# Engines of 708 operations from a table, and the low parts of two weight pieces on VectorE

## The chip, the cores and the metric

The kernel runs on one core of a Trainium2 chip. The metric is the device time of one execution in microseconds, lower is better.

## The reference

Three layers follow each other: attention with rotary positions (4 batches, 8 heads, 576 positions, 64 wide), a dense layer with a leaky ramp (2304 tokens, 512 to 2048 and back), and a soft mixture of 8 experts with 4 slots each. Cut to what is computed:

```python
q_rot, k_rot = rotate(q), rotate(k)
attn = softmax(scale * q_rot @ k_rot.T)
x = (attn @ v) as 2304 x 512
h = x @ w_in                                    # 512 -> 2048, weights given in 64 bits
x = (maximum(h, 0) + alpha * minimum(h, 0)) @ w_out
logits = x @ phi                                # 32 slots
d = softmax over tokens; slot_input = d.T @ x
slot_out[e] = maximum(slot_input[e] @ w1[e], 0) @ w2[e]
out = softmax over slots(logits) @ slot_out
```

## The kernel before

All work is cut into 2803 operations, each a few instructions on one engine, made by `plan.op(engine, cost, due, function, needed operations, buffers taken, buffers used)`. What fixes the order is not the due times but a table: `ORDER` is a packed list of all operations, which `Plan.order` unpacks and which is then issued from front to back. So the table sets what stands in each engine's own list; an engine works its list strictly in order and waits by semaphores for the others. DMA transfers are issued from SyncE's list in the same way.

**Attention.** For each batch `b` and pair of heads `p`, `prep_qk` loads q and k, multiplies by cos and sin (`mul`, L334) and adds (`add`, `whole`). In batch 0 scores are plain fp32 products (L434); from batch 1 on q and k are split into an fp32r part (`hi`, L350 and L352), its rest (`lo`, L357 and L359) and copies to the other partitions (`spread`, L362). `row_events` treats 128 rows at a time: scores on TensorE (L434, L443 to L447), the row maxima on VectorE (`top`, L452), the exponential with its sum on ScalarE (`expo`, L457), a guard of 1e-9 added to the sum (L473), the reciprocal (L474), and the product of the row with it, the norm (`norm`, L497 and L498). Batch 0 then turns blocks on TensorE (L521, L572) with evacuations (`turned`, L531; `turned_c`, L576); later batches turn 32x32 blocks on VectorE (L508, L542) and take a round trip through memory (tile `sc`). `pv_events` multiplies by v (L604) and evacuates a scaled fp16 part (`evac_hi`, L614) and its rest (`evac_lo`, L617).

**Weights.** `prep_w` loads a piece of `w_in` (8 pieces, `which` 0) or of `w_out` (8, `which` 1), converts it from 64 bits to fp32 by three VectorE operations (L673, L675, L677), and for `w_in` finds its bound (L685) and writes a scaled fp16 part (`hi`, L688). The low part comes from TensorE in two halves: `split` makes a diagonal of the scale (`diag`, L244), multiplies fp32 and subtracts the fp16 part in PSUM (L250, L251, tile `rest`), and evacuates (L256).

**The dense layer.** `chunk_events` runs `mm1` (L766, 12 fp16 matmuls of 128x256 for one of 16 chunks of one of 9 blocks of 256 tokens), the negative ramp `below` (L774) and the join `act` (L779). Its logits (L803), transposes of `g` (L795) and slot sums (L958) follow. The first `mm1` needs the attention of a quarter of batch 0; from there on chunks and score rows alternate on TensorE.

**Buffers.** There are two score banks (`st`) and three others (`pm`) in PSUM; a score bank is free after `expo`, the bank of a chunk after `act`. The weights of the experts (`late_w` and the loads behind it) need the attention's buffers, which are given back when its last operation, a `pv`, is done.

In the quoted functions engine and operation are fixed: the norm on `nc.gpsimd`, `below`, `evac_hi` and the guard on `nc.scalar`.

## Time and profile before

| | us |
|---|---|
| median of 3 runs (lowest, highest) | 570.95 (568.36, 573.3) |
| the profiled execution | 566.88 |
| its span | 565.1 |
| TensorE busy | 531.3 |
| VectorE busy | 449.7 |
| ScalarE busy | 348.8 |
| GpSimd busy | 321.9 |

Busy is the time in which at least one instruction of an engine runs; TensorE's are pipelined, and their ends are modelled. The trace has one line for each instruction with its start and duration. fp32 matmuls appear as two records. TensorE's clock was granted in full (0.996 on average). "Idle before" names what ended an engine's wait.

### The profile page before, as it was taken

What the parts mean: (1) busy time and instruction counts of PE and PEld (TensorE: products, weight loads), DVE (VectorE), ACT (ScalarE), POOL (GpSimd) and SP (SyncE); (2) the same over time, 40 slices, a digit from 0 to 9 for tenths busy, and PEclk for the clock granted to TensorE, in tenths of its full rate; (3) what the DMA queues carried; (4) which work ended last, traced back from release to release, by engine and by line L of the source; (5) the groups of instructions that cost most, each with busy time, mean ns of one, the idle gap of its engine ahead of it and who ended that gap; (6) DMA issues with size and microseconds to landing.
All of it is one profiled execution on the core that took longest, in us unless ns stands there. A gap on an engine that the chain in (4) does not pass through costs nothing.

```text
span 565.1 us, 14815 instructions
## 1 busy us (share of the span) xinstructions
PE 531.3 (94%) x5770; PEld 394.9 (70%) x5770; DVE 449.7 (80%) x985; ACT 348.8 (62%) x879; POOL 321.9 (57%) x299
## 2 busy tenths in 40 slices
PE   3789998999999999999999999999999999999994
PEld 1455555678888787788787788868778888864463
DVE  5699978878998878889889798888864799843551
ACT  2799977899868767787786787667432222430131
POOL 0989996988989876887886787844300000001000
PEclk9999999999999999999999999999999999999998
DMA  8893945435899988698989789889665999899997
GB/s 300 309 361 118 328 123 181 135 119 167 293 337 333 332 282 314 194 333 287 327 294 339 252 287 319 266 262 327 226 227 179 411 407 406 290 372 391 403 327 226
DMA packets 80806, 160.76 MB, mean 284 GB/s; under 512 B 5344, under 2 KB 44640, under 8 KB 80736
## 3 DMA queue, kind: packets, MB, share of 16 engines
q1 hardware_dynamic: 79408, 158.99, 80.6%
q8 instruction: 46, 0.75, 0.5%
q10 hardware_dynamic: 1328, 0.82, 0.5%
q14 instruction: 24, 0.20, 0.1%
HBM read 115.75 MB, written 36.96 MB: 270 GB/s over the span
## 4 chain that ended last, share of the span: by engine, by line
PE 75%; ACT 3%; DVE 2%; DMA 1%; issue 1%; DVEq 0%; ACTq 0%
PE ph L766 33%; PE pv L604 11%; PE st L447 9%; PE pu L958 4%; PE lg L803 3%; PE ph L1289 2%; PE po L1348 2%; DMA ett<-sc 1%; PE st L443 1%; PE pf L1473 1%; PE st L445 1%; PE pt L521 1%; PE lgt L863 1%; ACT ks L362 1%; ACT e L457 1%
## 5 line engine op out<-in xcount | busy, mean ns | idle before, releaser
L766 PE MATMUL ph<-xt,w 128*128 128x256 f16 x1536 | 184.2, 273 | 0.5 <-DVE xt L617 0.5
L766 PEld LDWEIGHTS <-w 128*128 128x128 f16 x1728 | 161.9, 98 | 30.2 <-issue 7.4
L498 POOL TENSOR_SCALAR e<-e,mm 128x576 f32<-128x576 f32 x144 | 125.5, 881 | 70.3 <-DVE mm L474 66.7
L457 ACT ACTIVATE e<-st,mm 128x576 f32<-128x576 f32 x144 | 106.3, 739 | 37.1 <-DVE mm L452 31.3
L452 DVE TENSOR_REDUCE mm<-st 128x1 f32<-128x576 f32 x144 | 106.2, 742 | 20.1 <-PE st L447 11.7
L774 ACT ACTIVATE rl<-ph 128x256 f32<-128x256 f32 x144 | 53.5, 380 | 69.7 <-PE ph L766 63.9
L334 POOL TENSOR_TENSOR xn<-xn,tabs 128x576 f32<-128x576 f32 x60 | 89.4, 1502 | 6.9 <-DMA xn<-in_k_dram 3.0
L779 DVE SCALAR_TENSOR_TENSOR g<-rl,oma,ph 128x256 f32<-128x256 f32 x144 | 65.7, 465 | 21.3 <-ACT rl L774 20.6
L604 PE MATMUL pv<-ET,vt 128*64 128x256 f32 (+1 forms) x640 | 76.5, 384 | 0.1
L508 DVE STREAM_TRANSPOSE tb<-e 128x512 f32<-128x512 f32 (+1 forms) x108 | 74.8, 704 | 1.7 <-DMA sc<-tb 0.8
L447 PE MATMUL st<-ks,qs 128*128 128x288 f32 x384 | 74.6, 317 | 1.1 <-ACT ks L362 0.9
L604 PEld LDWEIGHTS pv<-ET,vt 128*64 128x64 f32 (+1 forms) x640 | 43.1, 136 | 25.8 <-issue 5.8
L447 PEld LDWEIGHTS st<-ks,qs 128*128 128x128 f32 x384 | 54.5, 189 | 4.6 <-issue 1.6
L795 DVE STREAM_TRANSPOSE gb<-g 128x512 f32<-128x512 f32 x64 | 43.9, 693 | 0.2
L434 PE MATMUL st<-ks 64*128 64x288 f32 (+1 forms) x168 | 30.2, 455 | 11.0 <-DVE ks L307 7.6
L978 POOL MEMSET edt<- 128x256 f32 x1 | 0.3, 313 | 68.4 <-DVE lp L947 68.4
L359 POOL TENSOR_TENSOR qs<-xn,qs 64x576 fp32r<-64x576 f32 x24 | 33.9, 1413 | 7.7 <-ACT qs L352 3.1
L337 POOL TENSOR_TENSOR xn<-xn 128x576 f32<-128x576 f32 x24 | 36.9, 1537 | 0.9
L362 ACT ACTIVATE ks<-xn 64x576 fp32r<-64x576 f32 x48 | 32.6, 680 | 0.7
L434 PEld LDWEIGHTS st<-ks 64*128 64x128 f32 (+1 forms) x168 | 17.2, 191 | 20.8 <-DVE ks L307 8.4
L614 ACT ACTIVATE xt<-pv,vb 128x256 f16<-128x256 f32 x32 | 15.1, 472 | 22.3 <-PE pv L604 21.5
L457 ACT ACTIVATION_READ_ACCUMULATOR e<-st,mm 128x1 f32 x144 | 28.5, 198 | 0.0
(171 smaller groups left out, 782.1 us busy)
## 6 DMA issues: line engine op xcount, KB each, us to landing
sc<-tb SPq DMA_DIRECT2D x48, 576.0 KB, 4.6
ET<-sc SPq DMA_DIRECT2D x24, 1152.0 KB, 7.3
xw<-in_moe_w_dram SPq DMA_DIRECT2D x42, 512.0 KB, 8.4
xn<-in_k_dram SPq DMA_DIRECT2D x15, 576.0 KB, 6.5
xn<-in_q_dram SPq DMA_DIRECT2D x15, 576.0 KB, 4.5
wraw<-in_moe_w_in_dram SPq DMA_DIRECT2D x8, 1024.0 KB, 8.4
wraw<-in_w_out_t_dram SPq DMA_DIRECT2D x8, 1024.0 KB, 6.0
wor<-in_moe_w_out_dram SPq DMA_DIRECT2D x16, 512.0 KB, 10.0
```

The lines of the kernel that those rows point to most:

```text
L334: eng.tensor_tensor(e["x"][:, w], e["x"][:, w], tabs[:, w], ALU.mult)
L434: nc.tensor.matmul(st[to, j, at:at + w], x, k[rows, z:z + w], start=True, stop=True)
L447: nc.tensor.matmul(st[:, j, 0:288], r["q"][:, 768 * h + 128 * s:768 * h + 128 * s + 128].bitcast(F32R), r["k"][:, a, h, ks].bitcast(F32R), ...
L452: nc.vector.tensor_reduce(c["mm"][:, h:h + 1], c["st", h][:, :, 0:288], axis=AX.XY, op=ALU.max, negate=True)
L457: nc.scalar.activation(c["e"][:, h].rearrange("p (a n) -> p a n", a=2), c["st", h][:, :, 0:288], AF.Exp, bias=c["mm"][:, h:h + 1], accum_o ...
L498: nc.gpsimd.tensor_scalar(c["e"][:, h], c["e"][:, h], c["mm"][:, 6 + h:7 + h], 1.0, ALU.mult, ALU.mult)
L508: nc.vector.transpose(out=to if tail else to[:, :, 0:8].rearrange("p q (m h) j -> p q m h j", h=2)[:, :, :, h], in_=e.rearrange("p (m q j) ...
L604: nc.tensor.matmul(pv[r], v[k, 4 * h + i if i < 4 else 8 + (h if b else 0)], x, start=(i == 0), stop=(i == 4))
L766: nc.tensor.matmul(ph, wi[j][:, wp, kc, 128 * fo:128 * fo + 128], xt[:, xp, kc, :], start=(n == 0), stop=(n == 3 * KC - 1),)
L774: nc.scalar.activation(c["r"], c["ph"], AF.Relu, scale=-1.0)
L779: nc.vector.scalar_tensor_tensor(blk["g", j][:, fo, :], c["r"], oma[:, f:f + 1], c["ph"], ALU.mult, ALU.add)
L795: nc.vector.transpose(out=blk["gt", j // 2][:, f % 8 - 1:f % 8 + 1, :].rearrange("p c n -> p (c n)"), in_=blk["g", j][:, fo - 1:fo + 1, :] ...
```

## The change

A second table, `ENGINES`, holds one digit for each of 708 operations. `Plan.choose` takes the next digit and returns one of the engines that the call offers; `copied` and `times` write a copy or a product for whichever engine it is. So the following operations, which had one engine each, get the table's: diagonals and results of the splits, rotation products and sums, `hi`, `lo` and `spread` of q and k, guards, norms, the evacuations of the turned blocks, `evac_hi`, the scaled part of a `w_in` piece, and `below`. `ORDER` is a new list for the operations as they now are. Of the pieces of `w_in`, the last two (`j >= 6`) have no `split`: one VectorE operation (`lo` in `prep_w`, L747) multiplies the whole piece by its scale and subtracts the fp16 part. There are 2795 operations now. Over the whole program the table puts the 144 norms (those of the 16 short rows among them, each with a second instruction) on ScalarE (77), GpSimd (58) and VectorE (9), 33 of the 144 `below` and 18 of the 48 `evac_hi` on VectorE, 22 of 80 guards on VectorE, 42 of the 84 copies `hi` and `spread` on GpSimd and 3 on VectorE, and 8 products of the rotation on VectorE.

```diff
@@ -32,51 +32,58 @@
+ENGINES = (
+    "020000100000020000001200000011000202000020200020000100000100011000200100200102020002000110201110010002020002020001200000"
...
+)
...
-    "c-"
...
+    "c-m!F2S60p7M(k@EG!EPHbhX+1(hOL7BzrkR}3gbKvB?dVvIqPV2z>#HTGaHKbXXrh+s!WA^3xSno3j<umDPtA|OPOUUp~ZzxQSaFrP9r@3wR9edWGKE?G2it`A1#GTitFG?-"
...
+    def choose(self, *engines):
+
+        self.chosen += 1
+        return engines[int(ENGINES[self.chosen - 1])]
...
-    op = plan.op
+    op, choose = plan.op, plan.choose
     PE, ACT, DVE, POOL, DMA = "PE", "ACT", "DVE", "POOL", "DMA"
+    engines = {ACT: nc.scalar, DVE: nc.vector, POOL: nc.gpsimd}
+
+    def copied(on, dst, src):
+        if on == ACT:
+            nc.scalar.activation(dst, src, AF.Copy)
+        else:
+            engines[on].tensor_copy(dst, src)
+
+    def times(on, dst, src, scale):
+        if on == ACT:
+            nc.scalar.activation(dst, src, AF.Copy, scale=scale)
+        elif on == DVE:
+            nc.vector.tensor_scalar(dst, src, scale, None, ALU.mult)
+        else:
+            nc.gpsimd.tensor_scalar(dst, src, scale, 1.0, ALU.mult, ALU.mult)
+
     FIRST = -10000.0
...
+        on = choose(ACT, DVE, POOL) if dg[0] is None else None
+
+        def diag(on=on):
             e["d"] = wst.tile([128, 128], F32, tag="dg", name="dg", bufs=2)
-            nc.scalar.activation(e["d"], idf, AF.Copy, scale=scale())
+            times(on, e["d"], idf, scale())
 
...
-        o = op(ACT, 250, due, diag, [dep, neg_op], takes=[s_d], uses=[s_d]) if dg[0] is None else dg[2]
+        o = op(on, 250, due, diag, [dep, neg_op], takes=[s_d], uses=[s_d]) if dg[0] is None else dg[2]
...
-        return op(ACT, 595, due, lambda: nc.scalar.activation(dst(1), e["p", half], AF.Copy), [o, after], uses=[s_p] + uses)
+        on = choose(ACT, DVE)
+        return op(on, 595, due, lambda on=on: copied(on, dst(1), e["p", half]), [o, after], uses=[s_p] + uses)
...
-            def mul(w, e=e):
-                eng.tensor_tensor(e["x"][:, w], e["x"][:, w], tabs[:, w], ALU.mult)
-
+            def mul(w, on, e=e):
+                engines[on].tensor_tensor(e["x"][:, w], e["x"][:, w], tabs[:, w], ALU.mult)
...
-                    nc.scalar.activation(x[:, 1].bitcast(F32R), x[:, 0], AF.Copy)
+                    copied(on, x[:, 1].bitcast(F32R), x[:, 0])
...
-            o = op(on, cost, d, lambda mul=mul: mul(0), [o, *tabs_op], uses=[sx])
-            o = op(on, cost, d, lambda mul=mul: mul(1), [o], uses=[sx, s_tabs])
+            on = choose(POOL, DVE)
+            o = op(on, cost, d, lambda mul=mul, on=on: mul(0, on), [o, *tabs_op], uses=[sx])
+            on = choose(POOL, DVE)
+            o = op(on, cost, d, lambda mul=mul, on=on: mul(1, on), [o], uses=[sx, s_tabs])
...
-                    o = op(ACT, 640, d + LEADS[0], lambda hi=hi, h=h: hi(h), [o, y], uses=u)
-                    x = op(POOL, 1450, d + LEADS[0], lambda lo=lo, h=h: lo(h), [o, x if h else None], uses=u)
+                    on = choose(ACT, DVE, POOL)
+                    o = op(on, 640, d + LEADS[0], lambda hi=hi, h=h, on=on: hi(on, h), [o, y], uses=u)
+                    on = choose(POOL, DVE)
+                    x = op(on, 1450, d + LEADS[0], lambda lo=lo, h=h, on=on: lo(on, h), [o, x if h else None], uses=u)
...
-                        o = op(ACT, 640, d + LEADS[0], lambda spread=spread, h=h, up=up: spread(h, up), [o, y], uses=u)
+                        on = choose(ACT, DVE, POOL)
+                        o = op(on, 640, d + LEADS[0], lambda spread=spread, h=h, up=up, on=on: spread(h, up, on), [o, y], uses=u)
...
-        o = op(ACT, 75, n + LEADS[1] + hs - 1, lambda: nc.scalar.activation(c["mm"][:, 4:4 + hs], c["mm"][:, 2:2 + hs], AF.Identity, bias=eps[:, 0:1]), exps[-hs:], uses=[s_mm])
+        on = choose(ACT, DVE)
+
+        def guard(on=on):
+            to, of = c["mm"][:, 4:4 + hs], c["mm"][:, 2:2 + hs]
+            if on == ACT:
+                nc.scalar.activation(to, of, AF.Identity, bias=eps[:, 0:1])
+            else:
+                nc.vector.tensor_scalar(to, of, 1e-9, None, ALU.add)
+
+        o = op(on, 75, n + LEADS[1] + hs - 1, guard, exps[-hs:], uses=[s_mm])
...
-            def norm(h=h):
+            on = choose(POOL, DVE, ACT)
+
+            def norm(h=h, on=on):
                 if tail:
-                    nc.gpsimd.tensor_scalar(c["e"][:, 1, 0:64], c["e"][:, 0, 512:S], c["mm"][:, 6:7], 1.0, ALU.mult, ALU.mult)
-                nc.gpsimd.tensor_scalar(c["e"][:, h], c["e"][:, h], c["mm"][:, 6 + h:7 + h], 1.0, ALU.mult, ALU.mult)
-
-            o2 = op(POOL, 1200 if tail else 820, n + h + LEADS[1], norm, [rec[h]], uses=[s_mm, s_e])
+                    times(on, c["e"][:, 1, 0:64], c["e"][:, 0, 512:S], c["mm"][:, 6:7])
+                times(on, c["e"][:, h], c["e"][:, h], c["mm"][:, 6 + h:7 + h])
+
+            o2 = op(on, 1200 if tail else 820, n + h + LEADS[1], norm, [rec[h]], uses=[s_mm, s_e])
             norms.append(o2)
...
-                if h == 0 or not b:
-                    nc.scalar.activation(dst, src, AF.Copy)
-                else:
-                    nc.vector.tensor_copy(dst, src)
+                copied(on, dst, src)
...
-            evs.append(op(*((DVE, 690) if h and b else (ACT, 600)), n + h + LEADS[2], turned, [o2] + evs[:1], uses=[s_pm, s_ET]))
+            evs.append(op(on, 600, n + h + LEADS[2], turned, [o2] + evs[:1], uses=[s_pm, s_ET]))
...
-            nc.scalar.activation(dst(0), c["pv"], AF.Copy, scale=viv[b][:, 1:2])
+            times(on, dst(0), c["pv"], viv[b][:, 1:2])
...
-        def hi():
-            nc.scalar.activation(dst(0), xv(), AF.Copy, scale=sw[:, j:j + 1])
+        on = None if which else choose(ACT, DVE)
+
+        def hi(on=on):
+            times(on, dst(0), xv(), sw[:, j:j + 1])
+
+        def lo():
+            nc.vector.scalar_tensor_tensor(dst(1), xv(), sw[:, j:j + 1], dst(0), ALU.mult, ALU.subtract)
...
-        o = scaled = op(ACT, 1040, due + WS, hi, [o], uses=[s_wx, s_w])
+        o = scaled = op(on, 1040, due + WS, hi, [o], uses=[s_wx, s_w])
+        if j >= 6:
+            w_ops[0, j] = op(DVE, 1130, due + WS, lo, [scaled], uses=[s_wx, s_w])
+            return
...
-        def below():
+        on = choose(ACT, DVE)
+
+        def below(on=on):
             c["r"] = moe["p"].tile([128, 320], F32, tag="rl", name="rl", bufs=2)[:, 0:BLK]
-            nc.scalar.activation(c["r"], c["ph"], AF.Relu, scale=-1.0)
+            if on == ACT:
+                nc.scalar.activation(c["r"], c["ph"], AF.Relu, scale=-1.0)
+            else:
+                nc.vector.tensor_scalar(c["r"], c["ph"], -1.0, 0.0, ALU.mult, ALU.max)
 
         def act():
...
-        o = op(ACT, 385, d, below, [o], takes=[s_r], uses=[s_pm, s_r])
+        o = op(on, 385, d, below, [o], takes=[s_r], uses=[s_pm, s_r])
```

GpSimd, from its first norm on: before, it begins with the norms of the first rows (`e`) and the rotation products of later heads (`xn` by `tabs`).

```order
L498 TENSOR_SCALAR e<-e,mm 128x576 x2
L334 TENSOR_TENSOR xn<-xn,tabs 128x576 x4
L498 TENSOR_SCALAR e<-e,mm 128x576
L342 TENSOR_TENSOR ks<-xn 128x576
L498 TENSOR_SCALAR e<-e,mm 128x576
L334 TENSOR_TENSOR xn<-xn,tabs 128x576
L342 TENSOR_TENSOR ks<-xn 128x576
L498 TENSOR_SCALAR e<-e,mm 128x576 x2
L334 TENSOR_TENSOR xn<-xn,tabs 128x576
```

With the change:

```order
L366 TENSOR_TENSOR xn<-xn,tabs 128x576
L374 TENSOR_TENSOR ks<-xn 128x576
L225 TENSOR_SCALAR e<-e,mm 128x576
L225 TENSOR_SCALAR dg<-idf,sw 128x128
L366 TENSOR_TENSOR xn<-xn,tabs 128x576 x3
L374 TENSOR_TENSOR ks<-xn 128x576
L225 TENSOR_SCALAR e<-e,mm 128x64
L225 TENSOR_SCALAR e<-e,mm 128x576 x3
L374 TENSOR_TENSOR ks<-xn 128x576
L225 TENSOR_SCALAR e<-e,mm 128x576
```

Norms have left the list between the products, a diagonal (`dg`) has come in, and the sums (`ks`) follow sooner.

VectorE, from the conversion of the first piece of `w_in` (`w_163` before, `w_164` after, from `wraw`) on, before:

```order
L673 TENSOR_SCALAR w_163<-wraw 128x8x128
L675 SCALAR_TENSOR_TENSOR w_163<-wraw,w_163 128x8x128
L474 RECIPROCAL mm<-mm 128x2
L677 SCALAR_TENSOR_TENSOR w_163<-wraw,w_163 128x8x128
L452 TENSOR_REDUCE mm<-st 128x1 x2
L215 TENSOR_REDUCE mws<-top 128x1
L186 TENSOR_SCALAR mws<-mws 128x1
L187 TENSOR_SCALAR mws<-mws 128x1
L188 TENSOR_SCALAR inv_w<-mws 128x1
L474 RECIPROCAL mm<-mm 128x2
L189 RECIPROCAL sw<-inv_w 128x1
```

With the change:

```order
L727 TENSOR_SCALAR w_164<-wraw 128x8x128
L729 SCALAR_TENSOR_TENSOR w_164<-wraw,w_164 128x8x128
L731 SCALAR_TENSOR_TENSOR w_164<-wraw,w_164 128x8x128
L523 RECIPROCAL mm<-mm 128x2
L492 TENSOR_REDUCE mm<-st 128x1 x2
L223 TENSOR_SCALAR e<-e,mm 128x576
L366 TENSOR_TENSOR xn<-xn,tabs 128x576
L244 TENSOR_REDUCE mws<-top 128x1
L199 TENSOR_SCALAR mws<-mws 128x1
L523 RECIPROCAL mm<-mm 128x2
L200 TENSOR_SCALAR mws<-mws 128x1
L201 TENSOR_SCALAR inv_w<-mws 128x1
```

A norm and a rotation product stand between the maxima of the rows (`mm` from `st`) and the bound of the piece (`mws` from `top`).

TensorE, a place in the first stretch where the seventh piece of `w_in` (in `w_471`) gets its low part, before:

```order
L250 MATMUL rest<-w_471,dg 128x512
L251 LDWEIGHTS neg
L251 MATMUL rest<-w_471,neg 128x512
L250 MATMUL rest<-w_471,dg 128x512
L251 LDWEIGHTS neg
L251 MATMUL rest<-w_471,neg 128x512
L434 MATMUL st<-ks 128x288 x4
L727 MATMUL wpp<-w_748,phs 32x256 x4
```

With the change this piece (in `w_443`) has no `rest` on TensorE; VectorE has these rows, among the conversion of a piece of `w_out` (`w_719`) and the scale of another piece (`mws`):

```order
L727 TENSOR_SCALAR w_719<-wraw 128x1024
L523 RECIPROCAL mm<-mm 128x2
L729 SCALAR_TENSOR_TENSOR w_719<-wraw,w_719 128x1024
L747 SCALAR_TENSOR_TENSOR w_443<-w_443,sw 128x4x256
L199 TENSOR_SCALAR mws<-mws 128x1
L492 TENSOR_REDUCE mm<-st 128x1
```

The two splits of three TensorE rows each have become the one L747 row.

VectorE, among the first chunks of the dense layer, before, where `g` follows a `rl` that ScalarE makes:

```order
L675 SCALAR_TENSOR_TENSOR w_1321<-wraw,w_1321 128x1024
L779 SCALAR_TENSOR_TENSOR g<-rl,oma,ph 128x256
L452 TENSOR_REDUCE mm<-st 128x1
L474 RECIPROCAL mm<-mm 128x2
L779 SCALAR_TENSOR_TENSOR g<-rl,oma,ph 128x256
L452 TENSOR_REDUCE mm<-st 128x1
L474 RECIPROCAL mm<-mm 128x2
L677 SCALAR_TENSOR_TENSOR w_1321<-wraw,w_1321 128x1024
L452 TENSOR_REDUCE mm<-st 128x1
L779 SCALAR_TENSOR_TENSOR g<-rl,oma,ph 128x256
```

With the change, at some of the chunks:

```order
L559 STREAM_TRANSPOSE tb<-e 128x4x4x32
L841 TENSOR_SCALAR rl<-ph 128x256
L846 SCALAR_TENSOR_TENSOR g<-rl,oma,ph 128x256
L731 SCALAR_TENSOR_TENSOR w_1304<-wraw,w_1304 128x1024
L492 TENSOR_REDUCE mm<-st 128x1
L671 SCALAR_TENSOR_TENSOR xt<-pv,vb,xt 128x256
L559 STREAM_TRANSPOSE tb<-e 128x4x4x32 x2
L592 STREAM_TRANSPOSE tb<-e 128x4x32
```

L841 is `below`, now ahead of the join that reads it, in VectorE's own list.

## Rows read from the trace of the kernel before

**Rows 1.** The page: span, and busy time, share and instructions of each engine.

```profile
span 565.1 us, 14815 instructions
...
PE 531.3 (94%) x5770; PEld 394.9 (70%) x5770; DVE 449.7 (80%) x985; ACT 348.8 (62%) x879; POOL 321.9 (57%) x299
```

**Rows 2.** The page: shares of the chain that ended last, by engine.

```profile
PE 75%; ACT 3%; DVE 2%; DMA 1%; issue 1%; DVEq 0%; ACTq 0%
```

**Rows 3.** Busy time by stretch: us, each engine, TensorE clock, DMA share, GB/s.

```profile
0.00:122.60 122.60, 101.69 (x680) 60.70 (x681) 101.82 (x179) 96.95 (x230) 100.32 (x77) 1.00 0.66 227
122.60:208.90 86.30, 85.86 (x902) 70.22 (x901) 77.23 (x170) 66.54 (x168) 74.66 (x72) 1.00 0.80 273
208.90:419.50 210.60, 209.01 (x2481) 165.91 (x2481) 179.84 (x412) 146.00 (x384) 144.24 (x146) 1.00 0.86 288
419.50:503.00 83.50, 83.36 (x1008) 68.20 (x1007) 64.99 (x139) 26.52 (x73) 0.72 (x3) 1.00 0.88 332
503.00:565.10 62.10, 51.39 (x703) 29.84 (x702) 25.79 (x87) 12.79 (x29) 1.90 (x2) 0.96 0.94 339
```

**Rows 4.** TensorE in order of time: start, us; two splits, then the first `mm1`.

```profile
84.06 1.10 PE L250 MATMUL rest<-wx,dg 128*128 128x512 f32 x2
...
86.28 0.93 PE L521 MATMUL pt<-idf,e 128*128 128x128 f32 x7
...
122.73 1.47 PE L766 MATMUL ph<-xt,w 128*128 128x256 f16 x12
```

**Rows 5.** Busy time by stretch, near the end, columns as in Rows 3.

```profile
440.00:480.00 40.00, 40.00 (x483) 32.39 (x482) 36.87 (x79) 11.63 (x33) 0.00 (x0) 1.00 1.03 409
480.00:510.00 30.00, 29.11 (x365) 21.39 (x367) 19.71 (x46) 11.21 (x30) 0.72 (x3) 1.00 0.90 326
```

**Rows 6.** GpSimd by line (busy, mean ns | idle before): to 122.6 us, then 208.9 to 419.5.

```profile
L498 POOL TENSOR_SCALAR e<-e,mm 128x576 f32<-128x576 f32 x35 | 44.1, 1268 | 19.7 <-DVE mm L474 19.3
L334 POOL TENSOR_TENSOR xn<-xn,tabs 128x576 f32<-128x576 f32 x20 | 33.1, 1671 | 0.3 <-issue 0.3
...
L498 POOL TENSOR_SCALAR e<-e,mm 128x576 f32<-128x576 f32 x75 | 55.4, 749 | 42.2 <-DVE mm L474 39.7 <-ACT rl L774 1.0
```

**Rows 7.** ScalarE and VectorE by line, whole span: busy us, mean ns of one.

```profile
L350 ACT ACTIVATE xn<-xn 128x576 fp32r<-128x576 f32 x12 | 8.1, 677 | 0.3 <-POOL xn L337 0.3
L944 ACT ACTIVATE edt<-edt,vb 128x256 f32<-128x256 f32 x8 | 4.0, 497 | 0.0
L576 ACT ACTIVATE ET<-pc 128x128 f32<-128x128 f32 x16 | 4.4, 276 | 0.5 <-PE pc L572 0.3
L256 ACT ACTIVATE w<-rest 128x512 f16<-128x512 f32 x16 | 9.4, 587 | 0.5 <-PE rest L251 0.4
L774 ACT ACTIVATE rl<-ph 128x256 f32<-128x256 f32 x144 | 53.5, 380 | 69.7 <-PE ph L766 63.9 <-DVE wo L1128 2.2 <-DVE g L779 1.9
L302 DVE TENSOR_TENSOR xn<-xn,tabs 128x576 f32<-128x576 f32 x2 | 1.5, 758 | 4.9 <-DMA xn<-in_k_dram 4.1 <-DMA tabs<-in_rope_dram 0.8
L617 DVE SCALAR_TENSOR_TENSOR xt<-pv,vb,xt 128x256 f16<-128x256 f32 x32 | 14.8, 470 | 15.0 <-ACT xt L614 14.8
L474 DVE RECIPROCAL mm<-mm 128x2 f32<-128x2 f32 x64 | 9.3, 147 | 3.7 <-ACT mm L473 3.7
L1478 DVE COPY ob<-pf 128x256 f32<-128x256 f32 x2 | 0.8, 418 | 0.4 <-PE pf L1473 0.4
```

**Rows 8.** VectorE, the conversions: means to 122.6 us, then ns min/median/max of two lines.

```profile
L675 DVE SCALAR_TENSOR_TENSOR w<-wraw,w 128x1024 int32<-128x1024 int32 x11 | 16.9, 1541 | 0.2
L677 DVE SCALAR_TENSOR_TENSOR w<-wraw,w 128x1024 int32<-128x1024 int32 x11 | 16.0, 1450 | 0.0
L673 DVE TENSOR_SCALAR w<-wraw 128x1024 int32<-128x1024 int32 x11 | 11.4, 1040 | 1.3 <-PE wpp L727 0.8 <-DMA wraw<-in_moe_w_in_dram 0.5
...
L673 DVE TENSOR_SCALAR w<-wraw x12: 682/1074/1789, 12.6 to 122.9; 128x1024 int32<-128x1024 int32 x12
L675 DVE SCALAR_TENSOR_TENSOR w<-wraw,w x12: 1202/1612/1985, 13.3 to 125.7; 128x1024 int32<-128x1024 int32 x12
```

More of the change, by code (lines that the diff above doesn't have):

```diff
@@ L323, in prep_qk @@
             return
-        eng, on, cost = nc.gpsimd, POOL, 1570
+        cost = 1570
         for i, (src, z) in enumerate(((kx, "k"), (qx, "q"))):
@@ L331, in load, with add @@
                 nc.sync.dma_start(e["x"], src[b, p])
[L333 to L339 removed]
+            def mul(w, on, e=e):
+                engines[on].tensor_tensor(e["x"][:, w], e["x"][:, w], tabs[:, w], ALU.mult)
+            def add(on, e=e):
+                engines[on].tensor_tensor(e["x"][:, 0], e["x"][:, 0], e["x"][:, 1], ALU.add)
@@ L340, in whole, with hi @@
+            def whole(on, z=z, e=e):
                 if z == "k":
                     r["k"] = att.tile([128, 2, 2, S], F32, tag="K", name="ks", bufs=2)
-                eng.tensor_tensor(r["k"][:, 0, int(z == "q")], e["x"][:, 0], e["x"][:, 1], ALU.add)
+                engines[on].tensor_tensor(r["k"][:, 0, int(z == "q")], e["x"][:, 0], e["x"][:, 1], ALU.add)
             def half(w, h):
                 return slice(64 * (w ^ h), 64 * (w ^ h) + 64), slice((S + 128) * h, (S + 128) * h + S)
-            def hi(h=None, z=z, e=e):
+            def hi(on, h=None, z=z, e=e):
@@ L385, in prep_qk @@
                 continue
-            o = op(on, cost, d, add, [o], uses=[sx])
+            o = op(on, cost, d, lambda add=add, on=on: add(on), [o], uses=[sx])
             prev = order_ops.get(z)
@@ L622, in pv_events @@
         x.setdefault("op", o)
-        o = op(ACT, 130 if tail else 470, FIRST + n, evac_hi, [o, viv_op[b], x.get("first")], uses=u_)
+        o = op(on, 130 if tail else 470, FIRST + n, evac_hi, [o, viv_op[b], x.get("first")], uses=u_)
         x.setdefault("first", o)
```

131 lines of the change are left out of this document (68 added, 63 removed).

## The prediction

> **What bounds the kernel now.** I read the busy totals first [rows 1], then the chain that ended last [rows 2], then the busy time of every engine in five stretches [rows 3]. TensorE is busy 94% of the span and three quarters of the chain are its own work. The five stretches have different limits. In the first, up to the first chunk of `mm1` (its first matmul starts at 122.73 us [rows 4]), TensorE idles 122.6 - 101.7 = 20.9 us, and VectorE (101.8), GpSimd (100.3) and ScalarE (97.0) are about as busy as TensorE: no engine alone sets this stretch. From 122.6 to 503 us TensorE is busy 378.2 of 380.4 us, so the order of its own list is the time, and the others only have to keep up: VectorE does so with 77.2 of 86.3 us (89%), then 179.8 of 210.6 us (85%), then 65.0 of 83.5 us (78%). The last 62 us wait for the experts' weights: the loads can start only when the attention's buffers are given back, behind the last `pv` of attention, and from 440 to 480 us the DMA engines run at 409 GB/s, a share of 1.03 [rows 5]. Only between 480 and 510 us does the share fall, to 0.90.
>
> The profiled execution took 566.88 us, 1.8 us more than its span; the median of the runs before is 570.95 us, 1.0072 times that. I make the sum on the profiled execution and scale at the end.
>
> **The change, part by part.** (a) The last two pieces of `w_in` get their low part by one VectorE instruction each. TensorE loses four splits (one fp32 and one fp16 matmul of 512 columns each). Two splits in a row stand from 84.06 to 86.28 us [rows 4], 1.11 us each, so TensorE does 4.4 us less. All of that lies ahead of the first chunk in the list of before, where TensorE has 20.9 us to spare, so its worth lies between 0 and 4.4 us.
>
> (b) Ahead of the first chunk the new table has 35 norms on 12 GpSimd, 20 ScalarE and 3 VectorE; VectorE takes 7 of the rotation's products and 1 of its sums, GpSimd has 6 products fewer. The 35 norms cost GpSimd 44.1 us there, 1268 ns each, against 749 ns after 208.9 us [rows 6]; a product costs 1671 ns. GpSimd loses about 23 x 1.27 + 6 x 1.67 = 39 us of its 100.3 and stops being near the limit. ScalarE gains 20 norms. No row shows one: 128x576 without a scale takes 677 ns (L350), and 128x256 with a scale from memory 497 ns (L944), to which 320 more columns at (677 - 276)/448, from L576's 276 ns for 128 columns, add 286 [rows 7]. I take the mean of 0.68 and 0.78, 0.73 us; 14.6 us. It loses 27 small ones (5 `xt`, 5 diagonals, 5 results of the splits, 6 guards, 6 evacuations of transposes) at 0.28 (L576) to 0.59 us (L256), about 11 us, and 2 bounds and a scaled piece of 1024 columns, 1.08 us each by the same slope. ScalarE stays where it was, a little over 97 us.
>
> VectorE pays. It gains 7 products at 758 ns (L302, the same shape), two more of two inputs at the same price (a sum and a low part), 5 `xt` at 470 (L617 reads and writes the same shape), 3 norms, 5 guards at 147 (L474), the two new operations of a whole piece (the scaled piece and one low part: 0.68 and 1.20 us at best by L673 and L675 [rows 8]), 7 smaller evacuations at 0.28 to 0.69 and one more maximum, 0.75: 17 us. A norm on VectorE lies between 0.38 us (its part of 682 ns for 1024 columns, L673's fastest) and 0.76 (L302, two inputs); I take 0.42, near the lower, the operation being L673's. Successive VectorE instructions overlap by about 0.08 us in the trace, so 31 more cost 14 to 15 us.
>
> Something comes back. The conversions of the weights on VectorE take 1040, 1541 and 1450 ns on average in this stretch, and 682 and about 1202 (both of the others) at their fastest [rows 8]; for 15 pieces that is 14.2 us of excess, and the norms on GpSimd show its other side, 1268 against 749 ns. Both happen only where the two engines are busy at once. [...] VectorE: 101.8 + 14.5 - 5.5 + 2 = 112.8 us. Its first instruction waits 4.9 us for data (L302), so of 117.7 us it would be busy 96%, before 87%.
>
> So in this stretch one heavily loaded engine takes the place of another, and TensorE gets 4.4 us less to do. I take half of the 4.4, 2.2 us, as the gain.
>
> (c) From 122.6 to 208.9 us VectorE gains 7 `relu` out of PSUM, 3 `xt`, 5 guards, one low part of a piece, two small copies, and by the order three transposes of 512 columns more, which I price like a product, 0.7. A `relu` costs ScalarE 380 ns (L774); on VectorE no row has it, but a copy of the same shape out of PSUM takes 418 (L1478). Sum 9.2 us, less the overlap 7.5: 84.7 of 86.3 us, 98%. From 208.9 to 419.5 it gains 17 `relu`, 8 `xt`, 12 guards, 6 norms and two of the rotation, 11 us net: 190.8 of 210.6, 91%; after that 9 `relu`, two `xt` and a few steps, 5 us: 70 of 83.5. TensorE's own work there is the same 144 chunks, rows and transposed products; as long as VectorE is in time, these edits cost nothing, hidden behind TensorE. If the cover goes, each microsecond by which VectorE is over is one of the whole, since the maxima free the score banks and `g` frees the banks of the chunks.
>
> [...] The rows are fp32 out of PSUM, and there VectorE is no faster, 418 against 380 ns.
>
> GpSimd gains 42 copies of 64x576 in fp32r later on. Between a norm, 0.75 us, and a product of the first stretch, 1.67, they are 31 to 70 us, in place of the 63 norms (47 us) that it loses after 122.6; its 218.9 us of 296.9 become 203 to 242, which still leaves room. I take the norm's price, the operation having one input too.
>
> (d) The end moves with the last `pv`; the bytes are the same. The dip of the DMA share at 480 to 510 us is worth 30 x (1.03 - 0.90)/1.03 = 3.8 us at most. The order of the loads changes little; I count 1 us of it.
>
> Sum: 566.9 - 2.2 - 1.2 = 563.5 us for the profiled execution, 567.5 us on the scale of the median.
>
> **The rivals.** *The start really closes up* (faster). Against the sum above, VectorE might run without a pause, since ScalarE and GpSimd no longer hold its inputs up: then 4.9 + 112.8 = 117.7 us to the first chunk, and if all the excess of the conversions goes, 4.9 + 104.1 = 109. TensorE's own 97.3 us behind the same 4.9 us are 102.2. I take 113 to 117, 6 to 10 us gained, which reach the end whole, as the last `pv` and so the loads come earlier: 557 to 561, 561 to 565 on the median's scale. For it speaks GpSimd's relief of 39 us; against it that VectorE, ahead of the change, idled 21 us there while all its neighbours were under 83%.
>
> *VectorE becomes the bound after 122.6 us* (slower). It has 1.6 us left in 86.3. It decides from the point where the pauses that VectorE needs exceed those 1.6 us: before, it paused 9.1 us there. If a tenth of the time stays paused, 84.7/0.9 = 94.1, 8 us late by 208.9 us; the next stretch (91%) could add up to 4. That gives 575 to 579, 579 to 583 scaled. Against it: in the same place the new `relu` stand next to the `g` that waits for them, which takes one handover away.
>
> *The four splits are worth all of their 4.4 us and nothing else moves*: 562.5, 566.5 scaled; inside the likeliest case.
>
> **How the numbers follow.** The likeliest case, start nearly as long, TensorE unbroken, has 0.46 and the range 563 to 573; 0.04 of it lies more than 1% under 570.95 (565.2), 1% being about what a measurement of this kernel can tell from no change. The closed start has 0.32, VectorE as the bound 0.22. So faster 0.36, same 0.42, slower 0.22. The range for eight in ten runs from 557, a little under the closed start, to 580, the lower half of the slow case.
>
> **What would show it.** In the profile of the changed kernel: the first matmul of `mm1` at about 120 us (113 to 117 if the start closes); VectorE at 110 us or more and GpSimd near 60 in the time before it; the conversions at about 0.9, 1.4 and 1.35 us; a norm on ScalarE near 0.73 and a `relu` on VectorE near 0.42; TensorE with under 3 us of idle time from there to the fold, against 2.2 now. I am wrong if TensorE shows waits for the maxima or for `g` of more than 5 us in the 86 us after the first chunk, or if the copies on GpSimd are over 1.7 us and the scores wait for them.

## The result and the profile after

The changed kernel takes 571.89 us (median of 20 executions), the kernel before, measured beside it, 568.20. The ratio is 1.0067, 95% interval 1.0044 to 1.0090: slower by 3.7 us. That is inside the range, but on the other side of the kernel before: the forecast had it faster, 563.5 us against 566.9, a ratio of 0.9940.

The profiled execution of the changed kernel is the slowest of its 20 (577.0 us, against 566.88 us for the profiled one of before), so its losses are larger than those of the median: its trace shows where time goes, not how much a usual execution loses. The page, whose parts are those of [rows 1], with the line of the granted clock by slices:

```profile
span 575.2 us, 14748 instructions
...
PE 533.5 (93%) x5758; PEld 395.3 (69%) x5758; DVE 476.0 (83%) x1091; ACT 343.7 (60%) x827; POOL 259.4 (45%) x241
...
PEclk9999999999999999999998999999899999999997
...
q8 instruction: 45, 0.74, 0.5%
```

Busy time by stretch, cut at the same work as [rows 3] (the first chunk, the 31st, the 97th, the end of the chunks):

```profile
0.00:120.80 120.80, 98.01 (x669) 57.98 (x670) 105.57 (x209) 98.78 (x221) 63.98 (x50) 1.00 0.68 232
120.80:211.00 90.20, 88.40 (x908) 71.68 (x904) 81.29 (x189) 67.10 (x162) 65.09 (x63) 0.98 0.85 285
211.00:430.70 219.70, 212.84 (x2479) 167.15 (x2478) 195.61 (x459) 141.89 (x354) 127.03 (x125) 0.98 0.80 266
430.70:514.00 83.30, 83.30 (x1013) 68.40 (x1010) 68.61 (x150) 22.92 (x62) 1.43 (x3) 1.00 0.86 326
514.00:575.20 61.20, 50.94 (x703) 30.07 (x701) 24.92 (x87) 12.98 (x29) 1.91 (x2) 0.94 0.96 347
```

Against [rows 3] the start is 1.9 us shorter (the first chunk at 120.8, not 122.7 us), near the 2.2 forecast, and the tail 0.9 us. The second stretch is 3.9 us longer (90.2 against 86.3), the third 9.1 (219.7 against 210.6), and there the forecast had TensorE unbroken: its sign was under 3 us of idle time from the first chunk to the fold (the end of the chunks), and in the three middle stretches together it idles 8.7 us. VectorE is not at its limit in either: 81.3 of 90.2, 195.6 of 219.7 us.

What TensorE waited for between 120.8 and 514 us, in total, times, longest:

```profile
PE ph L828 <- DVE gb L862: 2.9, 1, 2.9
PE pu L1025 <- issue: 2.8, 3, 1.5
PE ph L828 <- issue: 2.7, 1, 2.7
PE pv L656 <- DMA ET<-sc: 0.3, 1, 0.3
```

The first three rows are five pauses, 8.4 us in all. Four carry "issue": TensorE waited for nothing that the profile shows. All five lie in or just behind `pu` (L1025), the slot product of a late block: 128 matmuls of 32x32, that is 256 instructions with their weight loads, in 2.7 us. TensorE around the second (start, us; idle before in brackets):

```profile
295.80 0.60 PE L656 MATMUL pv<-ET,vt 128*64 128x256 f32 x4
296.33 2.75 PE L1025 MATMUL pu<-gb,lp 32*32 32x256 f32 x128
299.01 0.80 PE L656 MATMUL pv<-ett,vt 128*64 128x64 f32 x20
302.68 2.74 PE L828 MATMUL ph<-xt,w 128*128 128x256 f16 x12 [2.87 <-DVE gb L862]
305.07 1.21 PE L487 MATMUL st<-ks,qs 128*128 128x288 f32 x6
```

The wait is put down to `gb`, but that transpose had ended at 301.82 us, 0.86 us earlier. In a run below (52 small matmuls) the same chunk starts at 298.61 us, before the same transpose has begun. The transpose in the changed kernel, then chunk and transpose in that run:

```profile
301.12 0.70 DVE L862 STREAM_TRANSPOSE gb<-g 128x512 f32<-128x512 f32 x1
```

```profile
298.61 1.48 PE L832 MATMUL ph<-xt,w 128*128 128x256 f16 x12
```

```profile
299.98 0.71 DVE L866 STREAM_TRANSPOSE gb<-g 128x512 f32<-128x512 f32 x1
```

The chunk at 302.68 takes 2.39 us to the next operation, not 1.24. The granted clock was 0.51 there, and 0.51 and 0.50 behind the pauses at 198.7 and 407.9 us, after TensorE had stood for 1.5 to 2.9 us:

```profile
199.60:203.00 3.40, 3.40 (x19) 1.95 (x20) 2.48 (x6) 0.22 (x1) 2.77 (x2) 0.51 1.00 346
...
302.00:305.40 3.40, 2.72 (x13) 2.04 (x14) 0.00 (x0) 0.00 (x0) 2.23 (x3) 0.51 1.00 384
...
407.90:411.30 3.40, 3.39 (x16) 2.53 (x16) 0.00 (x0) 0.21 (x1) 0.00 (x0) 0.50 0.99 283
```

Before, the clock was full from 122 to 503 us [rows 3].

**What the pauses have in common.** The page's `q8` row ("instruction") has 45 transfers of 16,384 bytes each (0.74 MB), about one for every 256 of TensorE's 11,686 recorded instructions, so I read it as the loading of these. In the trace's records every one of the five pauses ends at an instruction whose number is 193 more than a multiple of 256, 1.3 to 1.6 us after such a transfer has landed. I call the places 256 instructions apart borders, and what lies between two of them a block. A transfer started about when TensorE reached a border: over the 467 borders between 120 and 515 us in all thirteen traces, from 2.6 us ahead of that moment to 6.7 us behind it; and in the five pauses it was the transfer of the border before that had landed last. From this I infer that the transfer brings the block behind the next border, and that it had to arrive while the block before was worked off. Ordinary work mostly took 10 to 15 us for a block; one that `pu` fills for the most part took 2.7 to 5.9 without the pause. From the records of starts and transfers of the two profiled executions ("border reached" is the start of the block before the pause, "goes on" the start of the next; the share is that from the border to the start of the transfer, or, where the transfer started ahead of the border, that of the 1.5 us behind it):

| kernel | border reached, us | transfer starts / lands after it | TensorE goes on after | gap between starts | DMA share |
|---|---|---|---|---|---|
| after | 193.9 | 2.22 / 3.41 | 4.81 | 1.91 | 1.04 |
| after | 296.4 | 3.98 / 4.94 | 6.25 | 3.08 | 0.99 |
| after | 318.3 | 4.41 / 5.35 | 6.80 | 1.45 | 1.00 |
| after | 401.3 | 4.36 / 5.32 | 6.64 | 3.01 | 0.99 |
| after | 422.2 | 2.15 / 3.03 | 4.62 | 0.55 | 1.08 |
| before | 193.9 | -0.05 / 0.89 | no pause | 0.00 | 0.29 |
| before | 293.2 | -0.07 / 0.81 | no pause | 0.00 | 0.92 |
| before | 394.3 | 0.46 / 1.40 | 2.69 | 0.30 | 1.02 |

Before, three products of the eight (193.8, 294.6 and 394.3 us) fill a block nearly whole too, but their transfers started within 0.5 us. The 10.0 us of gaps and three half-clock stretches of 3.4 us, 1.7 us each, are 15.1; less 1.9 of the start, 0.9 of the tail and the wait of 1.3 us for `ett` that before had, 11 remain, against the 10.1 us between the two spans.

So theory I: the pauses are instruction loads. Theory II, what the forecast's slow rival says: the order and VectorE are late after the first chunk.

### The profile page after: what moved, and what is told of

Same layout as the page of the kernel before. It is cut to its first block, busy times and chain, and to the rows that moved or that the text cites. A ratio compares the mean times of both kernels' runs of the same rounds, so it can differ in the third digit from the quotient of the medians.

```text
span 575.2 us, 14748 instructions
## 1 busy us (share of the span) xinstructions
PE 533.5 (93%) x5758; PEld 395.3 (69%) x5758; DVE 476.0 (83%) x1091; ACT 343.7 (60%) x827; POOL 259.4 (45%) x241
## 4 chain that ended last, share of the span: by engine, by line
PE 75%; DVE 3%; DMA 2%; issue 2%; ACT 1%; DVEq 0%; ACTq 0%
PE ph L828 32%; PE pv L656 13%; PE st L487 9%; PE pu L1025 4%; PE lg L870 3%; PE po L1415 2%; PE ph L1356 2%; DMA ET<-sc 1%; PE st L483 1%; PE pf L1540 1%; PE st L485 1%; DMA sc<-tb 1%; PE lgt L930 1%; PE pt L572 1%; DVE mm L492 1%
## 5 line engine op out<-in xcount | busy, mean ns | idle before, releaser
L828 PE MATMUL ph<-xt,w 128*128 128x256 f16 x1536 | 186.9, 276 | 5.6 <-DVE gb L862 2.9
L366 POOL TENSOR_TENSOR xn<-xn,tabs 128x576 f32<-128x576 f32 x52 | 81.3, 1575 | 28.7 <-DMA xn<-in_k_dram 16.8
L225 POOL TENSOR_SCALAR e<-e,mm 128x576 f32<-128x576 f32 (+1 forms) x67 | 52.2, 783 | 84.4 <-DVE mm L523 79.7
L839 ACT ACTIVATE rl<-ph 128x256 f32<-128x256 f32 x111 | 41.3, 381 | 76.2 <-PE ph L828 71.1
L846 DVE SCALAR_TENSOR_TENSOR g<-rl,oma,ph 128x256 f32<-128x256 f32 x144 | 67.3, 472 | 15.2 <-ACT rl L839 14.1
L656 PE MATMUL pv<-ET,vt 128*64 128x256 f32 (+1 forms) x640 | 78.7, 391 | 0.3 <-DMA ET<-sc 0.3
L221 ACT ACTIVATE e<-e,mm 128x576 f32<-128x576 f32 (+1 forms) x83 | 60.3, 740 | 5.8 <-DVE mm L523 5.4
L369 POOL TENSOR_TENSOR xn<-xn 128x576 f32<-128x576 f32 x24 | 35.3, 1469 | 6.4 <-DVE xn L366 5.6
L572 PE MATMUL pt<-idf,e 128*128 128x128 f32 x144 | 22.8, 287 | 4.9 <-POOL e L225 3.6
```

The source lines that it names most:

```text
L221: nc.scalar.activation(dst, src, AF.Copy, scale=scale)
L225: nc.gpsimd.tensor_scalar(dst, src, scale, 1.0, ALU.mult, ALU.mult)
L366: engines[on].tensor_tensor(e["x"][:, w], e["x"][:, w], tabs[:, w], ALU.mult)
L656: nc.tensor.matmul(pv[r], v[k, 4 * h + i if i < 4 else 8 + (h if b else 0)], x, start=(i == 0), stop=(i == 4))
L828: nc.tensor.matmul(ph, wi[j][:, wp, kc, 128 * fo:128 * fo + 128], xt[:, xp, kc, :], start=(n == 0), stop=(n == 3 * KC - 1),)
L846: nc.vector.scalar_tensor_tensor(blk["g", j][:, fo, :], c["r"], oma[:, f:f + 1], c["ph"], ALU.mult, ALU.add)
```

## The experiments

**Moving the borders (five runs).** Small matmuls at the very start, in the 7 us in which TensorE waits for its first input, shift all borders without touching order or engines (44 in the first run, then 12, 108 and 52; in the kernel before 28):

```diff
                 for g in heads if 0 in js else ():
                     c["st", g] = ps_s.tile([128, 2, 512], F32, tag="st", name="st")
+                if early and 0 in js:
+                    some = idf[:, 0:64].bitcast(F16)
+                    for _ in range(44):
+                        nc.tensor.matmul(c["st", 0][:, 0, 0:32], some, some[:, 0:32], start=True, stop=True)
```

> The changed kernel with 44 small matmuls (88 TensorE instructions) more at its very start, where TensorE waits 7 us for its first input; their result is overwritten. Theory I (instruction loading): in the trace of the changed kernel TensorE's long pauses (198.7, 302.7, 325.2, 407.9, 426.8 us) all end at every 256th of its instructions, 1.3 to 1.6 us after a 16 KB transfer of its instruction queue, and in each the 256 short instructions of a slot product (`pu`, 2.7 us) fill most of such a block while the DMA engines are busy. 88 instructions more move the borders into the middle of the slot products; worked out from the trace with 5.5 us from border to border the pauses fall from 9.2 to 1.4 us. Expected: median 566 to 569, granted clock 0.993 or more, pauses of TensorE ending at a border under 2.5 us in all. Theory II (order and VectorE: the new table makes VectorE or its neighbours late after 122 us): order and engines are the same, so 571 to 573 as the changed kernel, with the clock at 0.985 to 0.99.

Measured: 567.25 us, ratio to before 0.9971 (0.9946 to 0.9996), as expected. 4.6 us under the changed kernel; granted clock 0.994 in the profiled execution, no half-clock stretch between the start and the tail. TensorE's waits from the first chunk to 500 us:

```profile
PE st L491 <- issue: 1.8, 1, 1.8
PE st L491 <- ACT e L501: 1.7, 2, 1.2
PE pv L660 <- DVE lp L1018: 0.9, 1, 0.9
```

Gaps at borders fell from 10.0 to 2.3 us (0.5 and 1.8). Theory II falls: it had 571 to 573.

> The changed kernel with 12 small matmuls (24 TensorE instructions) more at the same place: the control for the small matmuls themselves. Theory I: the slot products still fill most of a block (8.8 us of pauses against 9.2 worked out from the trace), so the time stays that of the changed kernel, 571 to 573. Theory II: the same, 571 to 573. If the small matmuls help by themselves (for instance by an earlier full clock), it comes out like the run with 44 of them.

Measured: 574.15 us, ratio 1.0095 (1.0062 to 1.0129), a little over the expectation. The same small matmuls at a bad place do not help. Pauses at 198.0, 300.8 and 406.3 us, at the borders of three of the changed kernel's five, 10.3 us in all, and half the clock behind the last two:

```profile
300.10:306.90 6.80, 6.07 (x36) 4.93 (x36) 1.49 (x3) 1.33 (x3) 1.89 (x2) 0.50 0.53 192
306.90:405.90 99.00, 95.40 (x1101) 76.10 (x1099) 90.62 (x211) 66.94 (x171) 56.19 (x57) 1.00 0.81 270
405.90:412.70 6.80, 6.43 (x29) 4.56 (x29) 2.05 (x5) 0.54 (x2) 0.00 (x0) 0.50 0.48 147
```

> The changed kernel with 108 small matmuls (216 TensorE instructions) more at the same place. Theory I: the worst place of the borders, 10.3 us of pauses worked out from the trace against 9.2 in the changed kernel: 572 to 574, and the pauses at other slot products than in the changed kernel. The 108 matmuls may not all fit into the first 7 us, which would add up to 2 us. Theory II: 571 to 573.

Measured: 569.52 us, ratio 1.0019 (0.9993 to 1.0045): a miss. One product did as expected (a gap of 3.8 us at 201.1 us, its transfer started 3.89 us after the border). Another, which fills 96% of its block, went through at 418 us; its transfer started after 0.5 us. In all its gaps at borders are 5.5 us, not the 10.3 worked out. How full a block is does not decide alone; the delay of its transfer decides with it, and the working with a fixed delay left that out.

> The changed kernel with 52 small matmuls (104 TensorE instructions): a second place of the borders for which the same working from the trace gives few pauses (2.0 us, against 1.4 with 44 and 9.2 without). Theory I: 566.5 to 569, clock 0.992 or more. If the run with 44 (567.25) was a lucky one and the place of the borders is not what counts: anything up to 572.

Measured: 566.11 us, ratio 0.9953 (0.9921 to 0.9985), 0.4 us under the range expected. **This version beats both kernels**, the one before by half a percent. Its busy time by stretch:

```profile
0.00:122.10 122.10, 102.32 (x720) 60.52 (x720) 105.56 (x209) 98.82 (x221) 63.96 (x50) 0.99 0.68 233
122.10:208.70 86.60, 86.31 (x908) 70.56 (x904) 81.06 (x189) 67.07 (x162) 65.07 (x63) 1.00 0.82 276
208.70:420.80 212.10, 209.46 (x2479) 165.48 (x2477) 195.54 (x459) 141.80 (x354) 126.83 (x125) 1.00 0.85 283
```

The second stretch is 86.6 us again, the third 212.1 (86.3 and 210.6 in [rows 3]), with VectorE as busy as in the changed kernel. Gaps at borders are 2.8 us in all. The clock of the profiled execution is 0.990, under the 0.992 expected: a half-clock stretch at 38.2 us lies in the start, and its first chunk comes at 122.1 us. From the first chunk to 500 us TensorE waits for nothing else but 0.7 us for scores:

```profile
PE pv L660 <- issue: 2.2, 2, 1.5
PE st L491 <- ACT e L501: 0.7, 2, 0.4
```

The profiled spans of the five kernels with this order (0, 12, 44, 52 and 108 small matmuls) go from 564.7 to 575.7 us. Less their gaps at borders and half of their half-clock time between the first chunk and the end of the chunks, they lie between 558.6 and 563.2: these two terms hold most of the difference.

> The kernel before with 28 small matmuls (56 TensorE instructions) more at the same place. Three of its slot products fill a block nearly whole (they begin 8 instructions ahead of a border, 23 and 1 behind one); its profiled execution shows no pause there, the transfers having been quick, but its other executions, up to 573 us, may. Theory I: the borders move into the middle of the products, 2.7 us of pauses against 7.5 by the same working, so the median falls by 1 to 2 us below the kernel before, the highest runs by more. Theory II: no change, ratio 0.999 to 1.001.

Measured: 570.47 us, ratio 1.0029 (0.9998 to 1.0060): a miss. The profiled execution of the kernel before loses 0.3 us at a border (the table above), so there was little to gain there; what its slower executions lose is not shown. In the profiled execution of this run the gaps at borders are 0.5 us and the loss lies in the start, where the first chunk comes at 126.4 us, 3.7 late, with two half-clock stretches (91.6 and 105.3 us). Why they fell there is open; the kernel before with 12 small matmuls (below) does not show them.

**Many short instructions on purpose.**

```diff
-            for k in range(0, 8, 2):
+            for k in (*range(0, 8, 2), *range(0, 8, 2)):
```

> The changed kernel with the 44 small matmuls (borders in the middle of the slot products), and each of the eight slot products of the late blocks made twice, the second overwriting the first: 256 short instructions more each, 2.05 thousand in all, which leave the borders where they are. Theory I (a block of 256 instructions is loaded only once TensorE has begun the one before, and takes 4 to 6.8 us until it can run): in 512 short instructions one block is always used up in 2.7 us, so beside the 8 x 2.7 = 21.6 us of work there are 2 to 4 us of pause at nearly every product, and half-clock stretches behind them: 567 + 21.6 + 14 to 35 = 603 to 624 us, with the clock at 0.985 or under. Rival (the pauses came from the order or the transfers alone, not from the number of instructions): 587 to 592 us, clock as before.

Measured: 611.29 us (two runs), ratio 1.075: 44 us over the same kernel without the doubling; the rival had 587 to 592. The profiled execution took 607.04 us, 39.8 over the profiled one without the doubling: TensorE is busy 26.2 us longer (21.6 us of work, the rest mostly three half-clock stretches that cost 1.7 us each) and waits 18.1 us, against 4.4 there. TensorE's waits from 120 to 540 us are all of one kind, and the product at 328.85 us shows it, 170 of its 256 matmuls and then the border:

```profile
PE pu L1029 <- issue: 18.1, 8, 3.7
```

```profile
328.85 3.63 PE L1029 MATMUL pu<-gb,lp 32*32 32x256 f32 x170
336.19 3.31 PE L1029 MATMUL pu<-gb,lp 32*32 32x256 f32 x86 [3.71 <-issue]
```

**Thinning the products out.** The first 64 matmuls stay, the rest follow one or two operations later, and the operations that need them are held back as long:

```diff
+            slots_half((0, 2))
+            second.append(lambda: slots_half((4, 6)))
...
+        if second and o.eng == PE:
+            passed = 0 if new else passed + 1
+            if passed == 2:
+                flush()
```

> The changed kernel without small matmuls; of each slot product of the late blocks the second half (64 matmuls) is issued only behind the next one or two operations in TensorE's list (a product with v, chunks), and what needs it goes behind it. Borders are not moved on purpose. Theory I: a block now holds other work beside the 256 short instructions, so it lasts 4 to 6 us at least, and most of the pauses go: 566 to 569.5 us, clock 0.992 or more. Rival (the place of the borders in the run with 44 small matmuls helped by another effect, or order and VectorE are what costs): 571 to 573, or more, as the gather of the product is later.

Measured: 576.05 us, ratio 1.0130 (1.0085 to 1.0176): a miss, though the gaps at borders fell from 10.0 to 3.9 us. TensorE's waits from 120 to 500 us:

```profile
PE st L487 <- DVE acc L1043: 3.2, 3, 1.1
PE pu L1032 <- issue: 3.2, 2, 2.1
PE st L487 <- DVE acc L1041: 1.2, 1, 1.2
```

The product holds both score banks, now for longer, and the scores wait for its gather (`acc`). These new pauses (4.4 us) stand next to what is left of the old ones, and the clock still falls to half (302.3 and 411.5 us). So this run does not tell the two theories apart by its time, only by its gaps.

**VectorE's share.** In the kernel with 44 small matmuls all `below` go back to ScalarE:

```diff
-        on = choose(ACT, DVE)
+        on = choose(ACT, DVE) and ACT
```

> The changed kernel with the 44 small matmuls and all 144 ramps `below` on ScalarE (33 were on VectorE): VectorE does some 12 us less after the first chunk. The forecast's step (edits on VectorE cost nothing as long as it is in time): 566.5 to 568.5, like the run with the 44 alone (567.25). The rival of the forecast (VectorE is the bound after 122.6 us): 563 to 565.5, as TensorE then no longer waits for it.

Measured: 569.29 us, ratio 1.0015 (0.9985 to 1.0044), against 0.9971 with the 33 `below` on VectorE. Relieving VectorE does not help; if anything it costs, 0.8 us beyond what was expected, and in the profiled executions most of that lies at the borders, where the gaps are 4.0 us here and 2.3 there. VectorE was not the bound: the rival had 563 to 565.5.

**Part (a) alone.** The low parts of the last two pieces on VectorE, in the kernel before:

```diff
+        def rest():
+            nc.vector.scalar_tensor_tensor(dst(1), src(), scale(), dst(0), ALU.mult, ALU.subtract)
+        if low:
+            diag = mults = lambda: None
...
-        return op(ACT, 595, due, lambda: nc.scalar.activation(dst(1), e["p", half], AF.Copy), [o, after], uses=[s_p] + uses)
+        return op(ACT, 595, due, rest if low else lambda: nc.scalar.activation(dst(1), e["p", half], AF.Copy), [o, after], uses=[s_p] + uses)
...
-                      lambda z, hh=hh: dst(z)[:, 2 * hh:2 * hh + 2], 512, "pm", scaled, [s_wx, s_w], o if hh else None, dg)
+                      lambda z, hh=hh: dst(z)[:, 2 * hh:2 * hh + 2], 512, "pm", scaled, [s_wx, s_w], o if hh else None, dg, low=j >= 6)
```

> The kernel before with one part of the change alone: the low part of the last two pieces of w_in comes from VectorE (in the two halves and at the places where the results of the splits were evacuated), not from TensorE. 12 small matmuls at the start replace the 24 TensorE instructions that fall out, so that the borders of the blocks stay. The forecast gave the four splits between 0 and 4.4 us and took 2.2 with the rest of the start: 564 to 568, against 568.0 before. If nothing of it reaches the end, 567.5 to 568.5; if the two more microseconds on VectorE make the start longer, 569 to 571.

Measured: 572.52 us, ratio 1.0074 (1.0042 to 1.0107), slower than any of the three cases expected.

> The kernel before with the 12 small matmuls at its start alone: the control for the run with the low parts on VectorE (572.5 us), whose profiled start was 2.2 us longer than that of the kernel before (first chunk at 124.9 against 122.7 us), as was that of the kernel before with 28 small matmuls (126.4). If the part itself makes the start longer: 567 to 569 here, first chunk near 122.7. If it is the small matmuls: 571 to 573 here, first chunk at 124.5 or later.

Measured: 568.89 us, ratio 0.9985 (0.9959 to 1.0011). So it is the part, not the small matmuls, at least in the order of the kernel before; what it is worth in the new order no run shows. The time to the first chunk, without the part and with it:

```profile
0.00:122.30 122.30, 103.45 (x694) 61.78 (x695) 101.01 (x179) 96.83 (x230) 100.30 (x77) 1.00 0.66 228
```

```profile
71.90:75.30 3.40, 3.33 (x9) 1.58 (x10) 3.36 (x4) 2.18 (x6) 3.40 (x3) 0.51 0.06 22
75.30:124.90 49.60, 43.55 (x355) 27.74 (x356) 42.32 (x65) 38.04 (x94) 42.02 (x30) 1.00 0.48 156
sum 124.90, PE 101.09 PEld 60.94 DVE 105.10 ACT 94.03 POOL 100.81; mean PE 33.70 PEld 20.31 DVE 35.03 ACT 31.34 POOL 33.60
```

TensorE has 2.4 us less to do, VectorE 4.1 more, and the start is 2.6 us longer; TensorE waits for VectorE (1.56 us ahead of 71.97 us) and then runs 3.4 us at half clock.

**Part (b) undone.** The norms of batch 0 back on GpSimd:

```diff
             on = choose(POOL, DVE, ACT)
+            on = on if b else POOL
```

> The changed kernel with the 44 small matmuls and the norms of batch 0 (those ahead of the first chunk among them) all back on GpSimd, where the kernel before has them. [...] Undone: conversions on VectorE back towards 1.04, 1.54 and 1.45 us, GpSimd back over 90 us of busy time ahead of the first chunk, and that chunk at 123 to 127 us against 120.9: 569 to 573. If GpSimd's part was of no weight: first chunk at 120 to 122, 566.5 to 568.5.

Measured: 578.75 us (five executions), ratio 1.0156 (1.0099 to 1.0212); the first chunk at 132.2 us, 11.3 later, more than expected. TensorE's longest waits until then, and GpSimd's norms:

```profile
PE pt L577 <- POOL e L225: 8.9, 5, 3.1
```

```profile
L225 POOL TENSOR_SCALAR e<-e,mm 128x576 f32<-128x576 f32 (+1 forms) x38 | 41.7, 1108 | 35.7 <-DVE mm L527 33.7 <-PE pc L627 1.6
```

GpSimd is busy 88.3 of 132.2 us, not full; the transposes wait for single norms, which take 1108 ns against ScalarE's 753 in the changed kernel, in an order made for norms on ScalarE. So the 11.3 us are the price of slower norms in this order, not what the move of the norms gained over the kernel before, whose own order had its first chunk at 122.7 us with all of them on GpSimd. Of the conversions two went only part of the way back (736 and 1270 ns, expected 1.04 and 1.54 us), the third past it (1558 ns, expected 1.45 us).

## Why the prediction was wrong

**What bounds the kernel** held: from the first chunk to the fold TensorE's list is the time. What failed is one term that the sum left at nothing, a half sentence of step (c): "TensorE's own work there is the same 144 chunks, rows and transposed products; as long as VectorE is in time, these edits cost nothing, hidden behind TensorE". VectorE was in time and the edits still cost: TensorE stood 8.4 us in five pauses that each ended 1.3 to 1.6 us after a transfer of `q8`, and the new order had moved its short instructions against the borders and against these transfers. In the profiled execution that term is 10.0 us of gaps at borders and 5.1 us of half clock behind them; in the medians, moving the borders alone takes the changed kernel from 571.89 to 566.11 us. The forecast named waits for `g` and maxima as what would show it wrong; the pauses came from neither. With few such pauses (52 small matmuls) the change gives 0.9953; the sum of the forecast is 0.9940.

That this is the cause is shown by the kernels with 44, 52 and 12 small matmuls and the doubled products, which change nothing but instruction counts (and, in the last, the work of the doubled products). That the full DMA engines delay the loads is argued from the traces and was not tried by itself. In the table the starts are 2 to 4.4 us after the border at shares of 0.99 to 1.08, -0.05 at 0.29, but also 0.46 at 1.02. Over the 467 borders of all traces the link is loose: where the share in the first microsecond behind the border was 1.0 or more, the transfer started 1.8 us after it in the median (233 borders, from -1.8 to 6.7), where it was under 0.3, 0.1 us ahead of it (57 borders, from -1.6 to 3.3). Why the transfers come late just at these products in the new order is not settled.

**(a)** Worth between 0 and 4.4 us, said the forecast. Alone, in the old order, it loses: 2.6 us at the first chunk, 3.6 in the medians (572.52 against 568.89). The lower bound of 0 left out that VectorE was 83% busy there and that others wait for its list. The operation itself was priced too low as well: a low part takes 1.77 us, not 1.20 at best.

**(b)** The start was to gain half of 4.4, 2.2 us: measured 1.9, and in eight profiled kernels with the new norms on ScalarE and the new order the first chunk comes at 120.0 to 122.1 us. That the size is right is luck: it was taken from TensorE's 4.4 us less work, which alone loses, while the relief of GpSimd was counted as taken by VectorE's new work. VectorE came to 105.6 us, not 112.8: the conversions fell to 693, 1231 and 1465 ns, so that of some 14 us of excess 10 came back, not 5.5. In the forecast's sum for VectorE the 5.5 us is an estimate (the 39% that GpSimd's busy time falls, taken of 14.2 us of excess) and the 2 us charged against it is a term that no run shows; what the runs showed in place of both is the 10 us. Against that a norm on VectorE took 876 ns there, not 0.42 us. In rows:

```profile
L727 DVE TENSOR_SCALAR w<-wraw 128x1024 int32<-128x1024 int32 x11 | 7.6, 693 | 0.0
L729 DVE SCALAR_TENSOR_TENSOR w<-wraw,w 128x1024 int32<-128x1024 int32 x11 | 13.5, 1231 | 0.1
L731 DVE SCALAR_TENSOR_TENSOR w<-wraw,w 128x1024 int32<-128x1024 int32 x11 | 16.1, 1465 | 0.1
L223 DVE TENSOR_SCALAR e<-e,mm 128x576 f32<-128x576 f32 x3 | 2.6, 876 | 0.0
L747 DVE SCALAR_TENSOR_TENSOR w<-w,sw 128x1024 f16<-128x1024 f32 x1 | 1.8, 1769 | 0.0
L221 ACT ACTIVATE e<-e,mm 128x576 f32<-128x576 f32 (+1 forms) x21 | 15.4, 753 | 1.0 <-DVE mm L523 0.9
```

The answering rows are [rows 8]; the norm on ScalarE, 0.75 us with its short ones, was forecast at 0.73. GpSimd is at 64.0 us (forecast about 61). That the new order rests on the norms' move is shown: undone, the first chunk is 11.3 us later. How much of the 1.9 us each part brings is not. That VectorE has 15 us of pauses left there and the start did not close up goes against the fast rival, as the forecast argued.

**(c)** The prices of the two main moves held: a `relu` on VectorE 409 ns (forecast 0.42), a copy on GpSimd 662 to 670 (forecast: the norm's 749).

```profile
L841 DVE TENSOR_SCALAR rl<-ph 128x256 f32<-128x256 f32 x33 | 13.4, 409 | 6.8 <-PE ph L828 6.5
```

```profile
L217 POOL CAST ks<-xn 64x576 fp32r<-64x576 f32 x21 | 13.9, 662 | 4.5 <-ACT xn L215 3.1 <-PE st L485 0.6
L217 POOL CAST qs<-xn 64x576 fp32r<-64x576 f32 x14 | 9.4, 670 | 0.7
```

VectorE is at 81.1 of 86.6 and 195.5 of 212.1 us where TensorE is hardly broken (52 small matmuls); forecast 84.7 of 86.3 and 190.8 of 210.6. The slow rival's time, 579 to 583, and its cause are both refuted: with VectorE at 94% of the second stretch, the waits of TensorE shown for that run name no VectorE instruction, and 0.7 us for scores is all that could come from VectorE by a detour.

**(d)** The tail gained 0.9 us. The forecast counts 1 us in the step and takes off 1.2 in the sum, a slip of 0.2 us that changes nothing here.

**The median against the profiled execution.** The scaling assumed one loss for all executions. The four of the changed kernel's 20 with a clock of 0.994 or more took 568.8 to 569.6 us, the three under 0.986 took 575.7 to 577.0: from which I read that the pauses come in some executions more than in others; only one of the 20 has a trace. Even those four lie over the median of the kernel before.

## What to carry to other kernels

When a new order leaves the engine that sets the time unbroken on paper, look at where its short instructions lie: here a run of some 250 of them was worked off in 2.7 us, while the next block took up to 6.8 us in the changed kernel until it could run, and a half-clock stretch came on top of three of the five pauses. Here such pauses were marked "issue", or had a releaser that had ended 0.86 us earlier, and ended 1.3 to 1.6 us after a transfer of `q8`; shifting the count of instructions in an idle place told them apart within one run (gaps at borders from 10.0 to 2.3 us). And a change that moves work to a busy engine can lose more than it saves elsewhere, even where the engine that it relieves is the busiest of all: here 2.4 us less on TensorE and 4.1 more on VectorE made the start 2.6 us longer.
